# K turned in 32 x 32 squares on VectorE, one V buffer, and scores in four column groups, in a single-token decode layer

## The chip, the cores and the metric

The kernel runs on one core of a Trainium2 chip. The metric is the device time of one execution in microseconds (us). The shorter names are those of the profile: PE is TensorE, DVE is VectorE, ACT is ScalarE, POOL is GpSimd, SP is SyncE, which here only issues the DMAs.

Times of different kernels are compared on the same chip, in the same rounds. A ratio is the mean time of one kernel's runs over that of the other's in those rounds, so it is not quite the ratio of the medians that are quoted.

## The reference

One token goes through attention over a long cache and through a gated MLP (cut to what matters; `x` is 1 x 640, 32 heads of 128, 4096 cached positions, bf16):

```
q = layernorm(x) @ wq                      # wq 640 x 4096
scores = q . k_cache * 128 ** -0.5         # k_cache 32 x 4096 x 128
o = softmax(scores) . v_cache              # v_cache 32 x 4096 x 128
h = x + o @ wo                             # wo 4096 x 640
n = layernorm(h)
out = h + (gelu(n @ w_gate) * (n @ w_up)) @ w_down     # 640 x 1728, 640 x 1728, 1728 x 640
```

K and V are 33.6 MB each, the weights together 17 MB. Each byte is used for one token only, so there is little arithmetic for each byte.

## The kernel before

The heads are taken in eight groups of four, called quads here. A quad's K is 4 MiB and so is its V. In SBUF each head has 32 partitions, with 128 cached positions of 128 numbers in each partition.

Scores need K with the head dimension on the partitions. The kernel before turns K on PE, in 128 x 128 blocks, into four PSUM banks; DVE and ACT copy the turned blocks back over K. Then each turned block is the stationary operand of one four-column matmul:

```python
def pe_transposes(slot, mark, after):
    ...
    for g in range(NG):                       # 16 groups of 8 blocks
        ...
        for b in range(GRP):
            inst = PE.transpose(
                tp_b[g % NBANK][:, b * DH : (b + 1) * DH], kt[slot][:, g * GRP + b, :], ident[:]
            )
        ...

def pe_scores(slot, half, ready, mark):
    for j in range(half * NB // 2, (half + 1) * NB // 2):
        ...
        inst = PE.matmul(s_ps[half][:, j % (NB // 2), :], lhsT=kt[slot][:, j, :],
                         rhs=q8[:, slot * QH : (slot + 1) * QH], start=True, stop=True)

def pe_pv(slot, half, mark):
    landed(f"v{slot}{'ab'[half]}")
    PE.wait_ge(S["act_pe"], EA_EXP[slot][half])
    for j in range(half * NB // 2, (half + 1) * NB // 2):
        inst = PE.matmul(o_ps, lhsT=vt[slot][:, j, :], rhs=e_t[:, j, :], start=(j == 0), stop=(j == NB - 1))
```

K has two buffers and so has V. The loads of one quad are issued together, as soon as the same buffer's last reader is done. The weights of `wo` go to an input tile first and POOL copies them on:

```python
def load_k(m):
    load_kv("k", m, kt, A_k_cache, m >= SLOTS and pe_at(m - SLOTS, ("s", 1)))   # SLOTS = 2

def load_v(m):
    load_kv("v", m, vt, A_v_cache, m >= SLOTS and pe_at(m - SLOTS, "pv"))

load("wq", wq_sb, ...)
load("x", ...)
for m in range(NQ):
    load_k(m)
    if m in (0, 2, 4):
        load_wo(m // 2)
    if m == 1:
        SP.wait_ge(S["q"], 1)
    load_v(m)
load_wo(TURNS - 1)
load("wg", ...)
load("wu", ...)
SP.wait_ge(S["pe"], pe_at(NQ - SLOTS, ("s", 1)))
load("wd0", ...)                      # 80 KB, then 1280, 480 and 320 KB of w_down
...
```

The softmax here doesn't subtract the row's maximum and nothing guards it: scores larger than these inputs give would overflow.

## Time and profile before

| | before |
|---|---|
| median of 6 runs | 206.16 us (205.93 to 206.55) |
| span of the profiled run | 204.3 us |
| bytes read | 84.23 MB |
| PE, DVE, ACT, POOL busy | 73%, 36%, 40%, 9% of the span |

The first lines are from the profile page of the kernel before: busy time of the engines, then two rows over the span cut in 40 equal slices. In the row "DMA" a digit is the mean busy share of the 16 DMA engines in tenths, and the row below has what they moved.

```profile
PE 148.2 (73%) x3425; PEld 136.6 (67%) x3427; DVE 73.6 (36%) x185; ACT 81.4 (40%) x179; POOL 19.1 (9%) x17
...
DMA  7999999999999999999999999999999999999991
GB/s 249 401 473 411 401 472 407 425 465 427 414 411 424 444 427 436 430 430 430 430 443 391 456 436 436 436 417 430 443 436 430 401 427 456 436 392 439 413 356 44
```

The DMA engines are busy in every slice but the first and the last. No compute engine is. The next two lines are a view of the same trace by windows (start and end in us, then each engine's busy time, PE's granted clock, the DMA's busy share, and GB/s):

```profile
1.50:190.00 188.50, 139.35 (x3279) 132.64 (x3284) 66.03 (x148) 81.19 (x178) 18.63 (x12) 0.79 1.00 428
190.00:201.00 11.00, 8.52 (x146) 3.88 (x139) 6.81 (x33) 0.21 (x1) 0.00 (x0) 0.94 0.86 337
```

The chain of waits of the kernel before, followed back from the last instruction, ends like this (start, duration, what):

```profile
167.65 33.31 DMA big<-in_B_w_down_dram
...
201.00 0.34 PE tp_105 L446 x8
...
201.36 0.33 DVE y_row L693
```

The last piece of `w_down` is issued at 167.65 and lands at 200.96 us; eight matmuls, one addition and the store of the result follow. So the kernel ends where its loads end. The groups of instructions that the change aims at were these (line, engine, operation, tiles, shape, count | busy us, mean ns | idle time before):

```profile
L252 PE MATMUL tp_103<-ident,big 128*128 128x128 bf16 x256 | 24.3, 251 | 11.8 <-PEq L176 11.8
L591 DVE COPY big<-tp_103 128x1024 bf16<-128x1024 bf16 x24 | 16.5, 688 | 19.5 <-PE tp_103 L252 19.5
L564 ACT COPY big<-tp_104 128x1024 bf16<-128x1024 bf16 x16 | 16.2, 1012 | 48.3 <-PE tp_104 L252 48.3
L265 PE MATMUL sb<-q_77,big 128*128 128x4 bf16 x512 | 14.3, 164 | 5.3 <-issue 5.3
```

### The profile page before, as it was taken

The page shows a single profiled execution, that of the slowest core. Times are in us where ns is not written, and L with a number is a line of the kernel's source. Part 1 is how long each engine was busy: PE and PEld are TensorE (multiplying, and loading weights), DVE is VectorE, ACT ScalarE, POOL GpSimd, SP SyncE. Part 2 cuts the span into 40 slices and gives each one's busy share as a digit, 9 for nine tenths or more (in the row PEclk, how much of TensorE's full clock was granted, in tenths as well). Part 3 has the DMA queues.
Part 4 walks back from the last instruction along what each step waited for, and adds up shares of the span by engine and source line. Part 5 has one row for each costly group of instructions (what it writes and reads, how often), then busy time and mean ns, then how long its engine had stood idle before and what let it go on. Part 6 is the DMA issues. An engine that isn't in the chain of part 4 may idle for free. (4 is left out here: it accounts for less than half of the span.)

```text
span 204.3 us, 7418 instructions
## 1 busy us (share of the span) xinstructions
PE 148.2 (73%) x3425; PEld 136.6 (67%) x3427; DVE 73.6 (36%) x185; ACT 81.4 (40%) x179; POOL 19.1 (9%) x17
## 2 busy tenths in 40 slices
PE   0001869845996499859985998389849989988963
PEld 0000259744996499859975997399749989987421
DVE  4006128300570059005701570048006801842481
ACT  0000137531476128614770567038703772773000
POOL 8300000620000000800000016000000000000000
PEclk9999969955698569856985698569856985995797
DMA  7999999999999999999999999999999999999991
GB/s 249 401 473 411 401 472 407 425 465 427 414 411 424 444 427 436 430 430 430 430 443 391 456 436 436 436 417 430 443 436 430 401 427 456 436 392 439 413 356 44
DMA packets 3963, 84.39 MB, mean 413 GB/s; under 512 B 464, under 2 KB 464, under 8 KB 752
## 3 DMA queue, kind: packets, MB, share of 16 engines
q1 hardware_dynamic: 3952, 84.23, 96.8%
q8 instruction: 8, 0.13, 0.3%
q14 instruction: 3, 0.02, 0.0%
HBM read 84.23 MB, written 0.00 MB: 412 GB/s over the span
## 5 line engine op out<-in xcount | busy, mean ns | idle before, releaser
L278 PE MATMUL o<-ex,big 128*128 128x4 bf16 x1024 | 29.8, 166 | 10.9 <-ACT ex L578 6.5
L278 PEld LDWEIGHTS o<-ex,big 128*128 128x128 bf16 x1024 | 28.4, 103 | 12.3 <-ACT ex L578 7.7
L564 ACT COPY big<-tp_104 128x1024 bf16<-128x1024 bf16 x16 | 16.2, 1012 | 48.3 <-PE tp_104 L252 48.3
L252 PE MATMUL tp_103<-ident,big 128*128 128x128 bf16 x256 | 24.3, 251 | 11.8 <-PEq L176 11.8
L252 PEld LDWEIGHTS tp_103<-ident,big 128*128 128x128 bf16 x256 | 19.9, 116 | 12.3 <-issue 12.3
L252 PE MATMUL tp_104<-ident,big 128*128 128x128 bf16 x256 | 23.6, 245 | 0.0
L591 DVE COPY big<-tp_103 128x1024 bf16<-128x1024 bf16 x24 | 16.5, 688 | 19.5 <-PE tp_103 L252 19.5
L511 POOL COPY wo<-wo_in 128x5120 bf16<-128x5120 bf16 x3 | 13.3, 4450 | 106.0 <-PE a L288 106.0
L252 PE MATMUL tp_105<-ident,big 128*128 128x128 bf16 x256 | 23.1, 242 | 0.0
L252 PE MATMUL tp_106<-ident,big 128*128 128x128 bf16 x256 | 22.7, 240 | 0.0
L252 PEld LDWEIGHTS tp_104<-ident,big 128*128 128x128 bf16 x256 | 19.3, 113 | 0.0
L252 PEld LDWEIGHTS tp_105<-ident,big 128*128 128x128 bf16 x256 | 18.9, 111 | 0.0
L252 PEld LDWEIGHTS tp_106<-ident,big 128*128 128x128 bf16 x256 | 18.7, 110 | 0.0
L265 PE MATMUL sb<-q_77,big 128*128 128x4 bf16 x512 | 14.3, 164 | 5.3 <-issue 5.3
L591 DVE COPY big<-tp_106 128x1024 bf16<-128x1024 bf16 x24 | 16.6, 691 | 2.9 <-PE tp_106 L252 2.2
L564 ACT COPY big<-tp_105 128x1024 bf16<-128x1024 bf16 x16 | 16.2, 1014 | 2.7 <-PE tp_105 L252 2.7
L265 PEld LDWEIGHTS sb<-q_77,big 128*128 128x128 bf16 x512 | 13.6, 96 | 5.5 <-issue 5.5
L578 ACT ACTIVATE ex<-sa 32x64 bf16<-32x64 f32 x32 | 9.8, 306 | 11.4 <-PE sa L265 11.2
L591 DVE COPY big<-tp_105 128x1024 bf16<-128x1024 bf16 x16 | 11.1, 692 | 8.4 <-PE tp_105 L252 8.1
L265 PE MATMUL sa<-q_77,big 128*128 128x4 bf16 x512 | 14.0, 164 | 0.0
L648 DVE COPY o_raw<-o 128x4 f32<-128x4 f32 x4 | 0.7, 162 | 36.7 <-PE o L278 36.7
L265 PEld LDWEIGHTS sa<-q_77,big 128*128 128x128 bf16 x512 | 13.5, 96 | 0.6
(113 smaller groups left out, 114.9 us busy)
## 6 DMA issues: line engine op xcount, KB each, us to landing
big<-in_A_v_cache_dram SPq DMA_DIRECT2D x8, 4096.0 KB, 33.4
big<-in_A_k_cache_dram SPq DMA_DIRECT2D x7, 4096.0 KB, 26.1
big<-in_A_wq_dram SPq DMA_DIRECT2D x1, 5120.0 KB, 15.4
wo_in<-in_A_wo_dram SPq DMA_DIRECT2D x4, 1280.0 KB, 27.2
big<-in_A_k_cache_dram SPq DMA_DIRECT2D x2, 2048.0 KB, 24.1
big<-in_B_w_gate_dram SPq DMA_DIRECT2D x1, 2160.0 KB, 39.2
big<-in_B_w_up_dram SPq DMA_DIRECT2D x1, 2160.0 KB, 44.3
big<-in_B_w_down_dram SPq DMA_DIRECT2D x1, 1280.0 KB, 32.3
```

The lines of the kernel that those rows point to most:

```text
L252: inst = PE.transpose(tp_b[g % NBANK][:, b * DH : (b + 1) * DH], kt[slot][:, g * GRP + b, :], ident[:])
L265: inst = PE.matmul(s_ps[half][:, j % (NB // 2), :], lhsT=kt[slot][:, j, :], rhs=q8[:, slot * QH : (slot + 1) * QH], start=True, stop=True,)
L278: inst = PE.matmul(o_ps, lhsT=vt[slot][:, j, :], rhs=e_t[:, j, :], start=(j == 0), stop=(j == NB - 1))
L511: POOL.tensor_copy(wo_t[:], wo_in[:]).then_inc(S["wo"], 1)
L564: ACT.copy(group(m % SLOTS, g), tp_g[g % NBANK]).then_inc(S["act_pe"], 1)
L578: inst = ACT.activation(e_t[r, cols, i], s_ps[half][r, :, i], AF.Exp, scale=SCALE, accum_out=rs_all[r, half, h : h + 1])
L591: DVE.tensor_copy(group(m % SLOTS, g), tp_g[g % NBANK]).then_inc(S["dve_pe"], 1)
L648: event(DVE.tensor_copy(o_raw[:, HG * turn : HG * turn + QH], o_ps))
```

## The change

DVE turns K from one SBUF buffer into another, in 32 x 32 squares of four-byte elements (two bf16 at a time), so that no PSUM bank and no copy is needed. The squares leave K in an order in which it can be the moving operand of 32 matmuls of 512 columns a quad; the query is the stationary operand, eight columns wide, and four such matmuls run at once in four column groups of 32. The scores of one quad then fit one PSUM bank. DVE turns them too, one exponential of 128 x 128 replaces eight of 32 x 64, and 16 small matmuls sort the result by heads.

SBUF is dealt out anew: two buffers for K as loaded, one for K turned, and one for V instead of two. K is loaded one quad ahead of V. `wo` is loaded straight into the tile from which it is used, each group behind V. The reciprocal root of the norms moves to POOL as a power. The core of the diff:

```diff
-    kt = [tile_at(i) for i in range(SLOTS)]
-    vt = [tile_at(SLOTS + i) for i in range(SLOTS)]
+    kr = [part(i * TILE, TILE) for i in range(SLOTS)]
+    vt = part(SLOTS * TILE, TILE).rearrange("p (j d) -> p j d", d=DH)
+    kt = part((SLOTS + 1) * TILE, TILE)
...
+    def pe_scores(mark):
+        for b in range(2):
+            PE.wait_ge(S["kt"], HALF * (b + 1))
+            for k in range(2):
+                for e in range(2):
+                    for r in range(4):
+                        inst = PE.matmul(
+                            s_bank[32 * r : 32 * r + 2 * QH, :],
+                            lhsT=q_quad[:, 2 * k + e, (1 - b) * QH : (3 - b) * QH],
+                            rhs=kt_at[:, k, HALF * b + r, :, e],
+                            start=(b, k, e) == (0, 0, 0),
+                            stop=(b, k, e) == (1, 1, 1),
+                            tile_position=(0, 32 * r),
+                        )
...
+    with nc.Fori(0, NQ, engines=only_pe):
+        mark = mark_at("quad")
+        pe_scores(mark)
+        PE.wait_ge(S["act_pe"], 1)
+        PE.sem_inc(S["act_pe"], -1)
+        pe_to_heads(mark)
+        PE.wait_ge(S["dve_pe"], 2)
+        pe_totals(t_ps, mark)
+        for half in range(2):
+            landed(f"v{'ab'[half]}")
+            pe_pv(half, mark)
+        ...
+        pe_project(mark)
...
+    def load_k(m):
+        if m >= SLOTS:
+            SP.wait_ge(S["dve"], D_SCORES[m - SLOTS])
+        load(f"k{m % SLOTS}", kr[m % SLOTS], rows_of(A_k_cache, m))
+
+    def load_v(m):
+        dst, src = vt.rearrange("p j d -> p (j d)"), rows_of(A_v_cache, m)
+        if m < NQ - 2:
+            if m > 0:
+                SP.wait_ge(S["pe"], pe_at(m - 1, ("pv", 1)))
+            load("va", dst, src)
+            SP.sem_inc(S["vb"], 16)
+        else:
             for h in range(2):
+                SP.wait_ge(S["pe"], pe_at(m - 1, ("pv", h)))
+                r = slice(h * TILE // 2, (h + 1) * TILE // 2)
+                load(f"v{'ab'[h]}", dst[:, r], src[:, r])
...
+    load_k(0)
     for m in range(NQ):
-        load_k(m)
-        if m in (0, 2, 4):
+        if m + 1 < NQ:
+            load_k(m + 1)
+        load_v(m)
+        if m % 2 == 1:
             load_wo(m // 2)
-        ...
...
+    def turn_keys(m, half):
+        to = kt.bitcast(f32).rearrange("p (k c j n) -> p c j k n", k=2, c=NC, n=HP)
+        of = kr[m % SLOTS].bitcast(f32).rearrange("p (c x) -> p c x", c=NC)
+        ...
+        for c in range(half * HALF, (half + 1) * HALF):
+            DVE.transpose(to[:, c], of[:, c].rearrange("p (j k n) -> p j k n", k=2, n=HP)).then_inc(S["kt"], 1)
```

In DVE's order the first half of the next quad's turns comes while PE waits for V, and the second half after the V matmuls. 
## The prediction

> **What bounds the kernel now.** The DMA. The DMA queue table gives 84.23 MB; the slice row has the DMA at 9 tenths or more in all slices but the first and last. Windows of the span: 428 GB/s from 1.5 to 190 us, 337 from 190 to 201. The Trainium skill, "DMA: Bandwidth & Descriptors", section "Where 436 GB/s comes from", puts the ceiling at 16 ports x 32 B x 850 MHz = 435.2 GB/s; this trace's 428 is 2% under it. The chain of waits ends in 33.3 us of w_down transfer (to 200.96), then 0.34 us of matmuls, 0.33 us of y_row and the store. No compute engine is full: PE 73%, ACT 40%, DVE 36%. The DMA queue's waits on PE pass with transfers already queued and cost no bandwidth.
>
> **Removed.** On PE 1024 transposes (23 to 24 us in each of four overlapping banks) and 1024 four-column score matmuls (28.3 us); the copies out of the transposes on ACT (48.6 us) and DVE (55.2 us); 32.4 us of 32-row exponentials and accumulator reads on ACT; the wo copies on POOL (13.3 us).
>
> **Added.** Eight DVE transposes of 1024 four-byte elements a quad. The trace's transposes out of PSUM took 605 ns for 416 elements and 208 for 64: 1.13 ns an element plus 0.14 us. Estimate: 1.3 us each, 10.4 us a quad. The Trainium skill, "Vector Engine (DVE) Microarchitecture Reference", section 3.8, says a transpose sustains one element per cycle per lane; the slope agrees (160 elements at a stride of five took 467 ns, but K is read contiguously). With the score turn, masks and small operations, 13 us of DVE a quad. PE: 32 score matmuls of 512 columns in four column groups; the query matmuls did 40 such in 4.1 us, so 3.3 us a quad.
>
> **The critical path.** The bytes are the same; the question is whether the DMA runs dry with V in one buffer. A quad's K, V and half a wo group take 21 us at 428 GB/s. From a V's landing: 3.7 us of V matmuls, 1.3 us to o_row, 5.2 us for the second half of the turns, 1.8 us scores, 0.7 turn, 0.4 exp, 0.6 to heads, 1.3 masks and totals: 15 us until the next V is usable, which lands after 20. V is reissued 4 us into a K transfer of 9.8 us; K after 12.5 us, with V in flight. So nothing runs dry, with 5 us to spare. At the head wq, K0, K1 and V0 (17.8 MB) last until about 43 us; K2 needs the first scores, by my sum at 39 to 41 us: a gap up to a microsecond is possible. At the end 7.9 MB follow V7, 18.5 us, against 8 us for the last attention and norm: the tail behind w_down stays.
>
> **Prediction.** 206.0 us, 8 in 10 between 204.6 and 208.0. Faster by over 2%: 0.05; within 2%: 0.84; slower by over 2%: 0.11.
>
> **What the profile would show.** 84.2 MB, still about 428 GB/s in the middle; PE busy near 75 us instead of 148; DVE up from 74 to 115; ACT below 12; POOL below 8; key turns of 1.2 to 1.3 us; the chain again ending in w_down and a 3.3 us tail.
>
> **What would make it wrong.** Turns of 2 us or more (DVE then needs 19 us a quad, and the chain from V to V passes 20): DMA slices below 8 tenths and some 215 us. Score matmuls that don't overlap. Late K2. Or a better rate with less PSUM copying, which I don't expect to exceed 2 us.

## The result, and the profile after

| | before | after |
|---|---|---|
| median | 206.26 us (20 runs, 205.93 to 207.0) | 206.61 us (10 runs, 205.85 to 208.43) |
| ratio to before, with 95% interval | | 1.0034 (1.0009 to 1.0058) |
| span of the profiled run | 204.3 us | 204.9 us |
| last piece of `w_down` lands | 200.96 us | 201.52 us |
| PE, ACT busy | 148.2, 81.4 us | 85.9, 4.6 us |

The busy times moved as the change wanted, and the time stayed within 2%. It rose by a third of a per cent, and the changed kernel's runs lie farther apart: of the 22 runs of it, 11 took 205.85 to 206.79 us and 11 took 207.18 to 208.52. The rise is mostly that second group: in the ten runs of the table the six of the low group have a mean of 206.28 us, and the 20 runs of the kernel before have the same 206.28. In the two later controls (experiments 1 and 9) the five low runs lie 0.1 to 0.6 us above it on the mean.

The same lines of the profile page, for the changed kernel:

```profile
PE 85.9 (42%) x1854; PEld 54.1 (26%) x1856; DVE 105.0 (51%) x184; ACT 4.6 (2%) x11; POOL 6.8 (3%) x12
...
DMA  7999999999999999999999999999999999999990
GB/s 248 416 456 409 416 461 448 416 416 446 448 413 434 436 416 416 441 461 416 416 406 464 416 441 461 416 416 422 418 446 441 413 419 361 416 421 432 423 373 26
```

One number stands out: 361 GB/s in the 34th slice, which is 169 to 174 us. The page's digits do not show it, because a slice of 5 us hides a gap of 1 or 2. The windows and the end of the chain of waits, as shown for before:

```profile
1.50:190.00 188.50, 77.33 (x1723) 50.12 (x1727) 98.92 (x158) 3.75 (x10) 5.70 (x6) 0.59 1.00 426
190.00:202.00 12.00, 8.61 (x140) 3.94 (x131) 5.35 (x23) 0.21 (x1) 0.55 (x1) 0.88 0.83 332
```

```profile
178.98 22.54 DMA big<-in_B_w_down_dram
...
201.56 0.34 PE y L362 x8
...
201.93 0.33 DVE y_row L596
```

The kernel still ends where its loads end, 0.56 us later (178.98 + 22.54 = 201.52). The new work, by groups:

```profile
L528 DVE STREAM_TRANSPOSE big<-big 128x1024 f32<-128x1024 f32 x64 | 73.7, 1211 | 4.2 <-issue 4.2
L260 PE MATMUL o<-ex,big 128*128 128x4 bf16 x1024 | 28.6, 166 | 43.2 <-PEq L167 43.2
...
L233 PE MATMUL s<-big,q_quad 128*8 128x512 bf16 x256 | 27.9, 580 | 21.4 <-DVE big L528 21.4
```

A turn of 1024 elements took 1.21 us. The second line is important for what follows: before its V matmuls PE sat idle for 43.2 us, in eight quads, because it waited for V to land (line 167 is the wait for a landing). Compute is ready 5.4 us a quad before its data.

Where is the slow slice? The windows of the changed kernel around it:

```profile
166.00:168.00 2.00, 0.65 (x25) 0.68 (x26) 2.00 (x2) 0.00 (x0) 0.00 (x0) 0.50 1.04 442
168.00:169.00 1.00, 1.00 (x43) 1.00 (x41) 0.24 (x2) 0.00 (x0) 0.00 (x0) 0.50 0.85 360
169.00:170.00 1.00, 0.20 (x8) 0.11 (x5) 0.00 (x0) 0.00 (x0) 0.00 (x0) 0.50 0.73 311
170.00:171.00 1.00, 0.00 (x0) 0.00 (x0) 0.00 (x0) 0.00 (x0) 0.00 (x0) 0.50 1.24 295
171.00:172.00 1.00, 0.00 (x0) 0.00 (x0) 0.00 (x0) 0.00 (x0) 0.00 (x0) 0.50 0.77 328
```

and the moment at which the first half of the last V is issued, in order of time (the V matmuls that must be done first, then SP's issue):

```profile
167.86 1.34 PE L260 MATMUL o<-ex,big 128*128 128x4 bf16 x45
...
169.23 0.33 SPq L431 DMA_DIRECT2D big<-in_A_v_cache_dram  x1
```

With one V buffer, the eighth quad's V may only be loaded when the seventh quad's V matmuls have read the old one. In earlier quads the next K is in the queue meanwhile and fills the 9.7 us. But K runs one quad ahead, so there is no K left after the eighth: the seventh V is followed by the eighth V directly. The change splits these two V in halves to soften that, but a break remains. Counting packets in half-microseconds, the 16 engines moved 306, 181, 244, 251 and 376 GB/s in the five half-microseconds from 169.5 to 172.0 instead of 430: a loss of 0.92 us on the mean of the engines. The texts that were put on record count quads from 0: their V6 and V7, or "the sixth quad's V and the seventh's", are the seventh and the eighth V here.

### The profile page after: what moved, and what is told of

It reads as the page before. It is cut to its first block, busy times and chain, and to the rows that moved or that the text cites. A ratio compares the mean times of both kernels' runs of the same rounds, so it can differ in the third digit from the quotient of the medians.

```text
span 204.9 us, 4113 instructions
## 1 busy us (share of the span) xinstructions
PE 85.9 (42%) x1854; PEld 54.1 (26%) x1856; DVE 105.0 (51%) x184; ACT 4.6 (2%) x11; POOL 6.8 (3%) x12
## 5 line engine op out<-in xcount | busy, mean ns | idle before, releaser
L528 DVE STREAM_TRANSPOSE big<-big 128x1024 f32<-128x1024 f32 x64 | 73.7, 1211 | 4.2 <-issue 4.2
L260 PE MATMUL o<-ex,big 128*128 128x4 bf16 x1024 | 28.6, 166 | 43.2 <-PEq L167 43.2
L233 PE MATMUL s<-big,q_quad 128*8 128x512 bf16 x256 | 27.9, 580 | 21.4 <-DVE big L528 21.4
L233 PEld LDWEIGHTS s<-big,q_quad 128*8 128x8 bf16 x256 | 7.0, 111 | 37.6 <-DVE big L528 29.3
L537 DVE STREAM_TRANSPOSE s_turned<-s 128x512 f32<-128x512 f32 x8 | 5.7, 717 | 13.5 <-PE s L233 13.5
L266 PE MATMUL a<-wo,o_row 128*1 128x160 bf16 x256 | 9.9, 333 | 2.3 <-DVE o_row L562 2.3
L540 DVE TENSOR_TENSOR ex<-e,of_head 128x512 bf16<-128x512 f32 x8 | 5.5, 692 | 6.8 <-PE e L248 6.8
L278 PE MATMUL t<-rs_cur,ones_f 128*128 128x4 f32 x16 | 4.7, 365 | 10.1 <-DVE rs_cur L548 10.1
L266 PEld LDWEIGHTS a<-wo,o_row 128*1 128x1 bf16 x256 | 7.1, 115 | 3.0 <-DVE o_row L562 3.0
L353 PE MATMUL s<-ex,ident 128*128 128x512 bf16 x12 | 4.2, 467 | 0.5 <-issue 0.5
L420 POOL MEMSET wo<- 128x5120 bf16 x1 | 4.4, 4368 | 0.0
```

What stands on the lines that cost most here:

```text
L233: inst = PE.matmul(s_bank[32 * r : 32 * r + 2 * QH, :], lhsT=q_quad[:, 2 * k + e, (1 - b) * QH : (3 - b) * QH], rhs=kt_at[:, k, HALF * b + ...
L260: inst = PE.matmul(o_ps, lhsT=vt[:, j, :], rhs=e_t[:, j, :], start=(j == 0), stop=(j == NB - 1))
L266: inst = PE.matmul(attn_ps[32 * r : 32 * r + 1, :], lhsT=o_row[:, j : j + 1], rhs=wo_t[:, j, r * YW : (r + 1) * YW], start=False, stop=j = ...
L278: mark("totals", PE.matmul(ps, lhsT=ones_f[:], rhs=rs_cur[:], start=True, stop=True))
L353: PE.matmul(s_bank[:], lhsT=ident[:], rhs=e_t[:].rearrange("p j h -> p (j h)"), start=True, stop=True)
L420: POOL.memset(t[:], 0.0).then_inc(S["pool"], 1)
```

## The experiments

Eleven kernels were run, each compared with the reference. All eleven passed, even the one that leaves the attention out (experiment 7): its share of this output is smaller than the tolerance, so the comparison says little about attention itself. Medians are of each run's own rounds; "before" in the same rounds was 206.13 us (first four), 206.24 (next three) and 206.27 (last four).

One more reading of the trace is used from here on. A load in this kernel is spread over all 16 DMA engines, and each raises the load's semaphore once when its share has landed. The Trainium skill, "DMA: Bandwidth & Descriptors", section "Why a DMA increments its semaphore by 16 and not by 1", says that only the full 16 mean that all data has landed. The trace agrees: it has 16 updates for each large load, and their times say when the first, the median and the last engine finished.

### 1. The changed kernel again

No edit.

> The changed kernel as it is, as the control on this chip. Theory 1 (the break): the time is that of the DMA's bytes, and the change costs a break of about 0.9 us in the DMA between the sixth quad's V and the seventh's, because V has one buffer and no K is left to fill the wait. Theory 2 (the rate): the key turns of VectorE in SBUF lower the DMA's rate by half a per cent all along. Both expect 206.6 us again, some runs near 208, ratio to before 1.002 to 1.006.

Measured: 208.15 us (206.74 to 208.52), ratio 1.007 (1.0042 to 1.0099). The higher group was the common one here, four of six runs, so that the median and the ratio lie above what was expected (206.6 us, 1.002 to 1.006). The profiled run took 208.52 us, and its last `w_down` landed at 203.26 us instead of 201.52. So the trace of this run can show what the high group is made of; see experiment 9.

### 2. Fill the break with w_gate

```diff
         if m + 1 < NQ:
             load_k(m + 1)
+        if m == NQ - 1:
+            load("wg", wg_sb, ...)
         load_v(m)
...
-    load("wg", wg_sb, ...)
```

> Changed kernel, with the load of w_gate (2.2 MB, 5 us, own region, no wait) moved between the last two V. Theory 1: the break is filled, the DMA keeps 425 to 432 GB/s there, and 0.9 us come back: 205.6 us, ratio to before about 0.997, and no runs near 208 if those are larger breaks. Theory 2: no change, 206.6 us.

Measured: 206.45 us (206.19 to 206.84), ratio 1.0012 (0.9997 to 1.0027). No run was near 208, and in the trace no half-microsecond between 5 and 190 us is below 410 GB/s. The second half of the expectation failed: 0.9 us did not come back, and the kernel is no faster than before. The last `w_down` landed at 200.96 us, just where it did before. On top, the end of the chain of waits had become compute:

```profile
200.21 0.20 DVE hid L595
...
200.45 1.43 PE y L362 x60
...
201.90 0.33 DVE y_row L597
```

With 2.2 MB less behind the last V, there is less time to hide the attention's end, the norm and the gate; `hid` was ready only at 200.4 us, and all 60 matmuls of `w_down` came after it. y_row starts 0.94 us after the landing (201.90 - 200.96), where it was 0.40 us in the kernel before (201.36 - 200.96). So with the break filled none of six runs was in the high group, and something other than the mean rate sets the landing.

### 3. Fill it with the last w_down rows as well

```diff
+        if m == NQ - 1:
+            SP.wait_ge(S["dve"], D_SCORES[NQ - SLOTS])
+            load("wd0", wd_last, ...)
+            load("wg", wg_sb, ...)
```

(and both taken out of their old places)

> As the last, and the 80 KB load of the last w_down rows, which goes to 32 partitions only, is moved with it, so that both fill the break. Theory 1: another 0.2 to 0.4 us, since the slump of the rate to 350 GB/s where this load runs beside the next w_down would then fall away from the end: 205.3 us. Theory 2: 206.6 us. If the slump moves with the load into the middle, it is that load's cost and the time is that of the last run.

Measured: 207.05 us (206.35 to 207.68), ratio 1.0034 (1.001 to 1.0059). A miss. The dip did move with the load of 80 KB into the middle, so that dip is the cost of this load, wherever it stands: 0.56 us of the DMA's mean was lost between 169.5 and 173 us. The last V then landed at 187.87 us, `hid` was ready at 201.4, and compute was again the end. The runs form two groups, three at 206.35 to 206.45 us and three at 207.64 to 207.68, though the break is filled. The profiled run is one of the slow ones, and its last `w_down` had landed at 201.24 us: there the time was lost to the late compute and not to the landing. The fast ones have no trace. Nothing is gained by moving the load.

### 4. Make the break larger

```diff
-        if m < NQ - 2:
+        if m < NQ:
             if m > 0:
                 SP.wait_ge(S["pe"], pe_at(m - 1, ("pv", 1)))
```

> Changed kernel with the last two V loaded whole instead of in halves: the break doubled several times over. Theory 1: V7 is issued only after V6 has landed whole and all 128 V matmuls are done (3.6 us), so the DMA stands still for about 6 us instead of 0.9: 211 to 212.5 us. Theory 2: 206.6 us.

Measured: 212.9 us (212.87 to 213.08), ratio 1.0327 (1.0313 to 1.0341), a little above the range of the expectation. The windows of this kernel show the break as a standstill of more than 4 us, with PE at the V matmuls that SP waits for:

```profile
168.00:170.00 2.00, 0.00 (x0) 0.00 (x0) 0.00 (x0) 0.00 (x0) 0.00 (x0) 0.50 0.73 311
170.00:172.00 2.00, 0.00 (x0) 0.00 (x0) 0.00 (x0) 0.00 (x0) 0.00 (x0) 0.50 0.08 33
172.00:174.00 2.00, 1.78 (x67) 1.81 (x68) 0.00 (x0) 0.00 (x0) 0.00 (x0) 0.50 0.00 0
174.00:176.00 2.00, 1.77 (x67) 1.68 (x64) 0.16 (x1) 0.00 (x0) 0.00 (x0) 0.50 0.00 0
176.00:178.00 2.00, 1.66 (x41) 1.28 (x45) 1.67 (x4) 0.00 (x0) 0.00 (x0) 0.50 0.92 262
```

So a break of the loads does reach the time. The mean of the engines lost 7.5 us here. On the slowest engine the sum is smaller: the seventh V's last landing is at 172.08, the eighth V of 4 MiB should follow 9.72 us later at 181.80, and it followed at 188.21 us. That is 6.4 us, and the time is 6.8 us above that of before. The standstill let the slow engines catch up: the last of the 16 landings was 2.15 us behind the first for the seventh V and 0.75 us for the eighth.

### 5. Two turns more in each quad

```diff
         for c in range(half * HALF, (half + 1) * HALF):
+            if half == 1 and c < HALF + 2:
+                wait(DVE, "xt", done["xt"])
+                tick("xt", DVE.transpose(scratch[:], of[:, c].rearrange(...)))
             DVE.transpose(to[:, c], ...).then_inc(S["kt"], 1)
```

> Changed kernel with two of the second half's four key turns done twice in each quad (the extra result goes to a scratch tile): 2.4 us more of VectorE on the way from one V to the next. If compute has slack there (PE waits for V 43 us in eight quads, 3 to 9 us each), the time stays within 0.5 us of 206.6. If compute or VectorE's SBUF traffic sets the time, it grows by up to 8 x 2.4 = 19 us, or by half a per cent more for the traffic alone (207.5).

Measured: 208.18 us (207.74 to 208.69), ratio 1.0083 (1.0062 to 1.0104). By the time alone this is a miss: all four runs lie where the high group lies. The trace says where it comes from. Up to the break nothing moved: the seventh V's last landing is at 172.01 us, against 172.09 and 171.96 in two traces without the extra turns. PE's wait for V shrank by just what was added:

```profile
L261 PE MATMUL o<-ex,big 128*128 128x4 bf16 x1024 | 28.6, 166 | 24.6 <-PEq L168 24.6
```

It was 43.2 us and is 24.6: 18.6 us less, which is 8 quads of 2.3 us. The extra turns were paid from slack. The rest is the break, which cost 2.9 us in the profiled run (the eighth V's end landed at 184.59 us, where 172.01 + 9.72 = 181.73 was due); the other three runs have no trace. Experiment 10 repeats this without a break.

### 6. All eight turns twice

The same edit with the condition always true.

> Changed kernel with all eight key turns done twice in each quad: 9.4 us more of VectorE, about 25 us a quad where the DMA needs 20.6. Slack theory: the slack of about 5 us is used up and some 4 us a quad come on top: 230 to 242 us, DMA slices below 9 tenths. A theory that compute does not matter at all: 206.6 us.

Measured: 237.87 us (237.42 to 238.13), ratio 1.1526 (1.15 to 1.1551), inside the range. The page's rows show a DMA that runs dry in each quad:

```profile
DVE  4021999689968996899689978997799869983242
...
DMA  7999999499999994899999967998999708999920
```

The slack is real and finite: the changed kernel can lose about 5 us a quad before the time notices, and then it notices every quad.

### 7. The loads alone

The loop over quads is taken out on all engines, so that the attention adds nothing to the output; this is wrong. The loads keep their order and, but for the last two V, which come whole and not in halves, their sizes; V gets two buffers, and a load waits for the landing of the load two before it:

```diff
     def load_v(m):
-        ...                                  # waits for the V matmuls
+        if m >= SLOTS:
+            arrived(f"v{'ab'[m % SLOTS]}")
+        elif m == 1:
+            SP.wait_ge(S["q"], 1)
+        dst = kt if m % SLOTS else vt.rearrange("p j d -> p (j d)")
```

> Wrong result on purpose: the same loads in the same sizes and order, with no attention work between; a load waits only for the landing of the load two before it in its buffer (V gets two buffers). Head and tail stay. Theory 1: 428 to 432 GB/s in the middle as in both kernels, no break, 205.0 to 206.0 us: nearly nothing of either kernel's time is compute. Theory 2: a higher rate in the middle, some 0.5 per cent above that of the changed kernel beyond the break, below 205 us.

Measured: 205.27 us (205.1 to 205.5), ratio 0.9953 (0.9934 to 0.9972). With no attention work at all the kernel is half a per cent faster than before. That is the most that a change of the attention's compute could have gained with these loads in this order; the head and the tail were left as they are.

It also settles the rival theory, that DVE's turns in SBUF take bandwidth from the DMA. In the middle of the span (45 to 165 us) the three kernels' windows, first before, then after, then the loads alone, are:

```profile
45.00:165.00 120.00, 98.02 (x2347) 95.95 (x2344) 43.92 (x84) 57.52 (x124) 8.97 (x4) 0.75 1.00 429
```

```profile
45.00:165.00 120.00, 54.37 (x1266) 36.57 (x1266) 65.81 (x99) 1.85 (x6) 0.00 (x0) 0.54 1.00 431
```

```profile
45.00:165.00 120.00, 0.00 (x0) 0.00 (x0) 0.00 (x0) 0.00 (x0) 0.00 (x0) 0.50 1.01 432
```

With 98 us of PE work or with none the rate is the same within 1%. The landings are sharper still: from one load of 4 MiB to the next of 4 MiB behind it, the last engine's landing moves on by 9.71 to 9.72 us in all three kernels, and so does the first engine's, outside the few loads in which the lag grows (below). That is 432 GB/s.

Why then is it 1.0 us faster than before? The semaphore updates of the traces (first engine / last engine, us):

```
                      w_q              fourth V          eighth V (its end)   last piece of w_down
before         15.07 / 16.32     98.95 / 100.97      179.82 / 181.84      198.95 / 200.96
after          15.09 / 16.13    105.57 / 107.58      180.91 / 182.49      200.10 / 201.52
loads alone    15.03 / 16.16    105.54 / 106.64      179.71 / 180.81      198.80 / 199.80
```

All engines run at the same rate, so an engine that has fallen behind stays behind while the queue is full. In the first load the last engine is 1.0 to 1.3 us behind the first. In the loads alone this lag stays at 1.1 us until the eighth V and is 1.0 at the end. In both other kernels it becomes 2.0 us. In the kernel before it stays so to the end; in the changed kernel the break deals it out anew, to 1.6 us for the eighth V and 1.4 at the end of this trace. Each time the end waits for the last engine. The time is thus the landing of the slowest engine, and a rest: in nine of the thirteen traces 5.1 to 5.3 us lie between the last landing (from the span's start) and the run's device time, and the other four are those whose compute at the end was late (experiments 2, 3, 6 and the second one of 10).

What makes the lag grow? In the trace of before seven packets of 16 KB on a queue of the kind "instruction" lie between 31 and 76 us, in that of after two, at 49.9 and 56.4 us, and in that of the loads alone none; each trace has one more within the last 6 us, and a few of 8 KB. In the changed kernel the lag of the last engine steps from 1.02 to 1.55 us in the load that spans the first and to 1.99 in the load that spans the second. The packets of the loads show it too: from 20 to 160 us eight packets of 32 KB in the trace of before and three in that of after took 1.63 to 1.88 us instead of 1.215, each starting 0.3 to 1.1 us after an instruction packet; the trace of the loads alone has none over 1.3 us. The Trainium skill, "Runtime: NRT & Kernel Launch", section "Instruction fetch mechanics", says that an engine's sequencer fetches its program in blocks of 16 KiB over its own DMA queue; the size of the packets and the kind of their queue agree with that. This link is read from traces and not from an edit; experiment 8 tests the other half, that a lag of one engine is what the time follows.

### 8. Hold one DMA engine up

The kernel before, with three loads of 34.6 KB into a single partition (a region that is still free), 0.12% more bytes:

```diff
     for m in range(NQ):
         load_k(m)
+        if m in (3, 4, 5):
+            lag(m > 3)      # waits for the last one's landing; one partition, one row
```

> Kernel before, with three loads of 34.6 KB more into a single partition (104 KB in all, 0.12 per cent of the bytes; meant to run on one DMA engine, 1.3 us each). Theory of the last engine: that engine falls 3.9 us back and, as it starts 0 to 2 us ahead of the last one, the end moves by 1.9 to 3.9 us: 208.0 to 210.0 us. Theory of the mean rate: 0.24 us more, 206.4 us.

Measured: 208.28 us (207.94 to 208.4), ratio 1.0089 (1.0072 to 1.0107). By the mean rate it should have been 206.5. The trace has each of the loads as one packet of 34.6 KB (1.28 to 1.29 us) with one update at its landing (and one 0.4 us after its issue, when the data was still queued), so each ran on a single engine. The landings of large loads, first engine / last but one / last, before the first and after each of the three:

```
K of the fourth quad      89.28 /  91.16 /  91.23
fourth V                  98.99 / 100.87 / 100.95
third group of wo        111.79 / 113.75 / 114.72
sixth V                  140.94 / 142.89 / 145.14
last piece of w_down     199.04 / 200.94 / 203.16
```

The first was swallowed by the lead that this engine had over the slowest one; the second put it 0.97 us behind the others, the third 2.25, and it carried the 2.2 us to the end. The chain ends with the landing at 203.16 instead of 200.96. So 104 KB cost 2.0 us in a kernel that moves 84 MB.

### 9. The changed kernel once more

> The changed kernel once more as the control of this chip: two modes, near 206.5 and near 208.2; in the profile the last V's last landing lies 0.6 us (fast) or 2.4 us (208) behind what the landings before the break promise.

Measured: 207.27 us (206.22 to 208.23), ratio 1.0035 (1.0003 to 1.0067), three runs in each group. The profiled run took 207.85 us. There are now three traces of the changed kernel, and the break can be measured on the slowest engine in each. Without a break the eighth V's end lands 9.72 us behind the seventh's:

```
run's time    seventh V lands    + 9.72     eighth V lands    lost     last w_down lands
206.65             172.09        181.81         182.49        0.68          201.52
207.85             172.01        181.73         183.55        1.82          202.60
208.52             171.96        181.68         184.23        2.54          203.26
```

The loss at the break and the end move together: 1.86 us between the first and the last row in the one, 1.74 in the other. So in these traces the high group is the break with a worse restart. When the break comes, all 16 engines have emptied their queues within 2 us, and their first packets of 16 KB afterwards mostly took 1.0 to 1.5 us instead of 0.61. That is so in the fast run too. In the four traces that have this break, what sets the dear ones apart is a second slow packet some 2 us after the restart: 1.6 and 1.8 us in the 208.52 run, 1.7 in the 207.85 run and 2.2 in that of experiment 5, against 0.93 at most in the fast run. Why such a packet comes in some runs these traces do not show.

### 10. A smaller filler, and the extra turns without a break

The break needs about 2 us of other bytes and not the 5 us of the whole `w_gate`:

```diff
+        if m == NQ - 1:
+            load("wg", wg_sb[:, 0:2], wg_rows[:, 0:2])      # 864 KB
         load_v(m)
...
-    load("wg", wg_sb, ...)
+    load("wgb", wg_sb[:, 2:DC], wg_rows[:, 2:DC])
```

> Changed kernel with only 864 KB of w_gate (two of five rows per partition, 2.0 us of DMA) moved between the last two V. Theory of the last engine: a load is usable when the slowest of the 16 DMA engines has landed its share, and a break costs the slowest engine 0.6 us (fast mode) or 2.4 us (mode of 208). The break is filled, and unlike with the whole w_gate the norm and gate chain after the last V is not pushed behind the DMA: the last w_down lands at 200.9 to 201.0, as in the kernel before, 206.1 us, ratio 0.999 to 1.001, no run near 208. Theory of the mean rate (my first one): 205.6 us.

Measured: 206.43 us (206.31 to 206.58), ratio 1.0003 (0.9988 to 1.0018). It is the changed kernel at its steadiest, with a range of 0.27 us: with experiment 2, twelve runs with a filled break and none in the high group. But the three low runs of the unfilled kernel in the same rounds (experiment 9) have a mean of 206.46 us, so to the good runs the filler gave nothing that shows in the time. The eighth V landed at 183.98 us, where 172.09 + 2.11 for the filler + 9.72 promise 183.92. The chain ends in the landing again and no longer in `hid`:

```profile
178.86 22.35 DMA big<-in_B_w_down_dram
...
201.25 0.47 PE y L362 x7
```

The landing at 201.21 us is 0.25 us behind that of before, and the median 0.16 us: the same time within the noise, though the landing is 0.2 us later than was expected. With the two extra turns in each quad on top of it:

> As the last, with two of the second half's four key turns done twice in each quad (2.4 us more of VectorE between one V and the next). Slack theory: as wg_part within 0.3 us, since the 208 of the run with the same extra turns came from the break. If the turns cost time or rate: 1.9 us above wg_part, as then.

Measured: 207.0 us (206.66 to 207.68), ratio 1.0038 (1.0013 to 1.0062). That is 0.57 us above the last, more than the 0.3 expected and far from 8 x 2.4. The landings are the same (fourth V 107.56 against 107.57, last `w_down` 201.28 against 201.21), so the turns still cost the DMA nothing. But in the last quad the slack is smaller than the added turns: V had landed at 184.12 us and its matmuls started only at 186.80 us, `hid` was ready at 200.69, and the end was compute, as in experiment 2. This is read from one trace; the other three runs have none.

No version beat both kernels. The best of the changed ones equals the kernel before, and the loads alone leave 0.5% to gain.

## Why the prediction was right, and where it was wrong

**The bound was right.** The kernel before ends with its loads, and so does the changed one. Taking 62 us from PE and 77 us from ACT (148.2 - 85.9, 81.4 - 4.6) changed nothing because neither was waited for. The loads alone, with no attention at all, are 0.5% faster; that was all there was to gain from attention.

**The costs of the new work were near.** Turns 1.21 us (predicted 1.2 to 1.3), DVE 105 us (115), ACT 4.6 (below 12), POOL 6.8 (below 8), and the score matmuls 27.9 / 8 = 3.5 us a quad (3.3). The slope of 1.13 ns an element for a PSUM source carried over to SBUF: eight turns back to back took 9.13 us, 1.11 ns an element. The Trainium skill, "Vector Engine (DVE) Microarchitecture Reference", section 3.8, was a good guide there: one element a cycle, with 0.96 GHz as "VectorE: DVE Perf Modes", section "Specifications", has it, is 1.04 ns as an estimate, and 1.11 was measured. PE was 85.9 us instead of 75. The projection now runs in every quad, with a zero row in half of them, and its 256 matmuls took 9.9 us where the kernel before had 160 in 4.1 us: about half of the difference.

**The slack of 5 us a quad was right.** PE waited 43.2 us for V in eight quads, 5.4 each. The runs with extra turns spent it: 2.3 us a quad came out of that wait one for one, and 9.4 us a quad overran it.

**The step that failed was "So nothing runs dry".** It was built on "V is reissued 4 us into a K transfer of 9.8 us", which holds for every quad but the last: no K follows the eighth, so the seventh and the eighth V stand next to each other and one buffer is not enough. The prediction looked for a gap at the head instead ("Late K2"); there K2 (the third quad's K) was issued at 37.88 us while V0 landed at 45.24, and no gap came. The break at the other end costs 0.7 us on the slowest engine in the one trace of the fast group and 1.8 to 2.5 us in the two of the high group. Filling it gave 206.43 us and left no high run in twelve.

**Some luck is in the number.** Eight of the 22 runs of the changed kernel took more than 208.0 us, the upper end of the range, and in the control of experiment 1 the median was 208.15. That the result's median was 206.61 depends on how many of its ten runs had the worse break, which nothing in the prediction foresaw.

**A step that was never tested by the prediction was the mean rate.** It read 428 GB/s for the DMA as if it were one pipe. The time follows the slowest of 16, and the rate and the lag are two different things: filling a break that cost the mean 0.92 us and the slowest engine 0.7 us moved the last landing by 0.31 us (201.52 to 201.21), and the time of the good runs by nothing that shows. Where the rest of the 0.7 us went these runs do not show.

**Open:** why the restart after the break is sometimes cheap and sometimes dear; and whether the instruction fetches alone make the lag grow from 1.0 to 1.3 us to 2.0, which the traces suggest and no edit isolated.

## What to carry to other kernels

Where the loads are busy from end to end, a faster compute engine is only worth the waits that end last, and a run with the loads alone tells beforehand how much that can be. When a buffer is given up because "the other stream covers the wait", check the ends of the loop, where the other stream has run out; a small load moved there is enough to keep the bad runs away, but not one so large that the tail behind it can no longer hide its compute. A load is as late as the slowest DMA engine, so look at the first and the last of the 16 landings and not only at GB/s.

## What the Trainium skill lacked or had wrong

- "DMA: Bandwidth & Descriptors" gives a rate for the DMA as a whole and one per engine, and says that two of the 16 are usually slower in traces. The runs show 16 engines with an equal rate (9.71 to 9.72 us per 4 MiB load for first and last alike) whose lags persist as long as the queue is full: 1.1 us in the loads alone, 2.0 us in both kernels (in the changed one until the break), and 34.6 KB on one engine set it back by 1.3 us for good. No page that was read says that the end of a load-bound kernel is set by such a lag.
- "Runtime: NRT & Kernel Launch", section "Instruction fetch mechanics", calls the cost of crossing a 16 KiB boundary mostly hidden. For the sequencer that may be so; here each fetch packet took 1.0 to 1.1 us, a packet of 32 KB beside one took up to 1.88 us instead of 1.215, and the lag of the last engine grew by 0.5 and 0.4 us at the two fetches of the changed kernel.
- "DMA: Bandwidth & Descriptors" has a first-byte latency of about 0.6 us for the hardware path and does not say from when it counts. The first packet at 170.18 us came 0.95 us after the start of the issue (169.23) and 0.62 us after its end (169.56), so it agrees if counted from the end. The page has nothing on a restart: the first packets of 16 KB after a break took 1.0 to 1.5 us instead of 0.61.
- "DMA: Bandwidth & Descriptors" has no number for a load into 32 partitions beside others: the 80 KB load of the last `w_down` rows came with a loss of about 0.4 to 0.6 us of the DMA's mean wherever it stood, where its bytes alone need 0.2.
